# Turning four x tiles by one DMA and moving two v projections and one k projection in a fused attention and GEGLU kernel

## The chip, the cores and the metric

The kernel runs on one core of one Trainium2 chip. The metric is the device time of one execution in microseconds (us), lower is better. Most executions of one kernel lie within 0.3 to 0.4% of each other here, so most kernels were executed five times, in rounds shared with the kernel before on the same chip. All executions compared are in the fast state, with a granted clock of 1.0.

## The reference

Two branches share one input x of 2048 rows and 640 columns (bfloat16), and a gate mixes them.

```python
g = sigmoid((x * gate_w).sum(-1, keepdims=True))
# a: linear attention, 32 heads of 20 columns
q, k, v = split(x @ wqkv)                            # 640 x 1920
pq, pk  = q @ w_phi, k @ w_phi                       # per head, 20 x 20
phi_q   = concat(softmax(pq), softmax(-pq)); phi_k = the same of pk
kv = einsum(phi_k, v); z = sum(phi_k)
a  = ((phi_q @ kv) / (phi_q @ z + 1e-6)) @ wo
# b: GEGLU feed-forward, 1728 inner columns
b  = (gelu(x @ w_gate) * (x @ w_up)) @ w_down
out = g * a + (1 - g) * b
```

## The kernel before

It is one long hand-ordered program. TensorE (PE) multiplies; VectorE (DVE) and ScalarE (ACT) move results out of PSUM ("evict" them), whose banks 0 to 7 the program hands out by hand; SyncE (SP) issues nearly all DMAs. The 2048 rows are 16 tiles of 128 rows. Only the first 30 us matter here.

The projections read x transposed, from SBUF (`xT`). PE transposes tiles 0 to 3, transposing DMAs do the rest (`xturn(t, n)`: n tiles from tile t). w_phi is multiplied into the weights of k and q once ("folds"): for this, wk and wq come transposed as well (`wload`), and each of five folds of one weight is written to a pair of banks and evicted by DVE ("d") or ACT ("a").

The DMAs on SP's queue, in order of issue:

```python
xload("sp", 0); xload("sp", 2)                 # rows of tiles 0 to 3, plain
for kt in range(KD):                           # wv, five plain DMAs
    sc.dma("sp", ... self.w3[:, kt, 0:D] ...)
xturn(4, 2)
wload(self.wkT, D, "wkT")
xturn(6, 2)
wload(self.wqT, 0, "wqT")
xturn(8, 4)
xturn(12, 4)
# ... plain loads of w_gate, w_up, w_down, wo
```

The order of PE's work after v of tiles 0 to 3 (`ve(t, b)`: v of tile t into banks b, b+1, evicted by ACT; `ke`: k, followed by two exps on ACT; `f(kt, which, banks, engine)`: a fold):

```python
ve(4, 6)
ve(5, 0)
f(0, "k", (2, 3), "d")
f(1, "k", (4, 5), "a")
f(2, "k", (6, 7), "d")
f(3, "k", (0, 1), "a")
f(4, "k", (2, 3), "d")
ve(6, 4)
ke(0, 6)
self.k_sums(0)            # DVE: the softmax sums of tile 0, one TENSOR_REDUCE
ve(7, 0)
ke(1, 2)
f(0, "q", (4, 5), "d")
f(1, "q", (6, 7), "d")
ke(2, 0)
f(2, "q", (4, 5), "d")    # "the third q fold": needs banks 4, 5 of the first one back
f(3, "q", (2, 3), "d")
self.proj(3, 640, 384, 6, 128, ["wk2"])        # first half of k of tile 3
f(4, "q", (4, 5), "d")
self.proj(3, 1024, 257, 7, 0, ["wk2", "wgate"])
self.k_evac(3, 6)
self.k_scale(0)
self.k_norm(1)
self.pq(0, 1, 1, 0) ...   # pq = x @ folded wq
self.gram(0)              # phi_k^T v of tile 0, needs the scaled exps of tile 0
# ... then tiles 4 to 15: k (and v), pq, gram of an earlier tile
```

The softmax here doesn't subtract the row's maximum and nothing guards it: scores larger than these inputs give would overflow.

Of the kernel before, what the change touches and what calls it, by code (L numbers as in the profile page):

```python
# [107 lines left out]
class _Kernel:  # L108
# [99 lines left out]
    def loads(self):  # L208
# [10 lines left out]
        def wload(T, c0, key):  # L219
            sc.dma("sp", lambda e: e.dma_start_transpose(T[:, :, :], self.wqkv[:, c0:c0 + D]), writes=[key])  # L220

        def xturn(t, n):
            a, z = t * P, (t + n) * P
            sc.dma("sp", lambda e: e.dma_start_transpose(self.xT[:, :, a:z], self.x[a:z, :]),
                   writes=[("xT", k) for k in range(t, t + n)])
# [8 lines left out]
        xload("sp", 2)  # L234
        for kt in range(KD):
            sc.dma("sp", lambda e: e.dma_start(self.w3[:, kt, 0:D], w3[:, kt, 2 * D:3 * D]), writes=[("wv", kt)])
        xturn(4, 2)
        wload(self.wkT, D, "wkT")
        xturn(6, 2)
        wload(self.wqT, 0, "wqT")  # L240
        xturn(8, 4)
        xturn(12, 4)
# [308 lines left out]
    def attention_state(self):  # L551
        NT = self.NT
        order = [(b, i) for b in range(self.NB) for i in range(self.KD)]
        sc = self.sc
        ones = self.nc.const_aps.tensor(1.0, [P, 512], BF16)
        for n in (512, 512, 512, 512, 512, 512, 128, 128, 128):
            sc.op("pe", lambda e: e.matmul(self.bank(0, n), ones[:, 0:P], ones[:, 0:n], start=True, stop=True),  # L557
                  writes=[("ps", 0)])
        vs, ve, xt = self.v_step, self.v_first_evac, self.x_transpose
        xt(0, "d")  # L560
        xt(1, "a")
        for i in range(3):
            for a, b in ((0, 2), (64, 3)):
                sc.op("pe", lambda e: e.matmul(self.bank(b, P), ones[a:a + 64, 0:P], ones[a:a + 64, 0:P], start=True,  # L564
                                               stop=True), writes=[("ps", b)])
        xt(2, "d")
        xt(3, "a")
        for t in range(4):
            vs(t, 0)
        for t in range(4):  # L570
            vs(t, 1)
        for t in range(4):
            vs(t, 2)
        for t in range(4):
            vs(t, 3)
        self.blockdiag()
        self.gate_column(6)
        for t in range(4):
            vs(t, 4)
            ve([t], "ad"[t % 2], False)  # L580
            if t == 2:
                ve([0, 1, 2], "a", True)
        ve([3], "d", True)
        f = self.fold
        ve, ke = self.v_early, self.k_early
        ve(4, 6)
        ve(5, 0)
        f(0, "k", (2, 3), "d")
        f(1, "k", (4, 5), "a")
        f(2, "k", (6, 7), "d")  # L590
        f(3, "k", (0, 1), "a")
        f(4, "k", (2, 3), "d")
        ve(6, 4)
        ke(0, 6)
        self.k_sums(0)
        ve(7, 0)
        ke(1, 2)
        f(0, "q", (4, 5), "d")
        f(1, "q", (6, 7), "d")
        ke(2, 0)  # L600
        f(2, "q", (4, 5), "d")
        f(3, "q", (2, 3), "d")
        self.proj(3, 640, 384, 6, 128, ["wk2"])
# [5 lines that stand above are left out]
        self.pq(0, 1, 1, 0)  # L609
        self.pq(0, 0, 0, 1)  # L610
        self.pq(0, 3, 3, 2)
        self.columns = True
        self.gram(0)
        self.k_norm(2)
        self.pq(0, 2, 2)
        self.k_norm(3)
        n = 4
        g = 1
        for t in range(4, NT):
            if t < 8:  # L620
                self.k_early(t, 1)
            else:
                self.vk(t)
            self.k_norm(t)
            m = 2 * t - 2 if t < 8 else t + 5
            while n < m:
                if n == m - 1:
                    for g in range(g, t - 2):
                        self.gram(g)
                    g = t - 2  # L630
                self.pq(order[n][0], order[n][1], n)
                n += 1
# [242 lines left out]
```

## Time and profile before

| | before |
|---|---|
| median of 3 executions | 286.44 us (286.05 to 287.1) |
| span in the profile | 285.0 us |
| PE busy | 281.1 us, 99% |
| x tiles 4, 5 issued, landed, read | 4.10, 8.57, 10.8 us |
| wk issued, landed, read | 5.90, 12.84, 13.5 us |
| x tiles 6, 7 issued, landed, read | 9.45, 13.99, 15.3 us |
| sum of tile 0 on DVE | 19.72 to 21.20 us |
| third q fold starts | 22.77 us |

Landings are the time when the last of the increments of the DMA's semaphore arrives; the traces show sixteen for each of these DMAs (those of x tiles 4 and 5, for one, between 8.50 and 8.57 us). The page of the kernel before, its busy times and the chain of work that ended last:

```profile
...
PE 281.1 (99%) x3045; PEld 186.1 (65%) x3060; DVE 174.4 (61%) x352; ACT 105.2 (37%) x200; POOL 5.3 (2%) x36
...
PE 99%; issue 0%; ACT 0%
PE ps L361 62%; PE ps L737 28%; PE ps L681 2%; PE ps L373 2%; PE ps L468 2%; PE ps L341 1%; PE ps L557 1%; PE ps L298 0%; ACT outsb L750 0%; PE ps L564 0%; PE ps L323 0%
...
```

PE is the chain, from end to end. A busy PE isn't a full PE, because the profile models the ends of matmuls; so the thing to read is the distance between starts. In the stretch of interest 512-column matmuls start every 215 to 216 ns and 128-column ones every 55 ns. I call a "hole" what the distance between two starts has over that. Whatever delays PE here delays the end, unless it is made good later, and PE has hardly a hole in which to make it good.

The timeline of the kernel before (start in us, duration in us, engine, line, operation, out<-in, count; in brackets the idle time of the engine before it and what ended it). SPq is SP's sequencer issuing a DMA; the duration is that of the issue. L361 is a projection, L341 a fold, L438 the softmax sum, L354 the eviction of a fold. `ps` is PSUM, `xT`, `wkT`, `wqT` what the transposing DMAs bring, `BD` w_phi spread for the heads, `Ek` the exps of k, `Dk` their sums:

```profile
...
4.10 1.76 SPq L224 DMA_TRANSPOSE xT<-in_A_x_dram  x1
...
5.90 3.50 SPq L220 DMA_TRANSPOSE wkT<-in_A_wqkv_dram  x1
...
9.45 1.40 SPq L224 DMA_TRANSPOSE xT<-in_A_x_dram  x1
...
11.04 2.66 PE L361 MATMUL ps<-w,xT 128*128 128x512 bf16 x19
...
13.54 1.96 PE L341 MATMUL ps<-BD,wkT 128*128 128x140 bf16 x30
...
15.55 5.39 PE L361 MATMUL ps<-w,xT 128*128 128x512 bf16 x39
...
19.72 1.49 DVE L438 TENSOR_REDUCE Dk<-Ek 128x64 f32<-128x1280 bf16 x1 [3.29 <-ACT gcol L426]
...
20.78 0.79 PE L341 MATMUL ps<-BD,wqT 128*128 128x140 bf16 x12
...
21.36 1.56 DVE L354 CAST wq<-ps 128x640 bf16<-128x640 f32 x2 [0.16 <-PE ps L341]
...
22.77 0.79 PE L341 MATMUL ps<-BD,wqT 128*128 128x140 bf16 x12
...
25.33 3.19 PE L361 MATMUL ps<-xT,wq 128*128 128x512 bf16 x14
...
```

Neither a DMA nor an eviction is named as releaser before any PE group. (Some matmul records are missing, so a group can seem to start one matmul late, as at 11.04.) The sum of tile 0 is done at 21.20, and the first q eviction at 21.36 waits for PE. How long the first turning DMA took from issue to landing (view of one tile, `xT`, in the window of that issue; the three numbers of the first line are the duration of the issue in ns, those of the second the time to landing in us):

```profile
...
L224 SPq DMA_TRANSPOSE xT<-in_A_x_dram x1: 1760/1760/1760, 4.1 to 4.1; - x1
...
DMA to landing us min/median/max: 4.5/4.5/4.5
```

### The profile page before, as it was taken

To read this page: it belongs to the slowest core of one execution; us is meant where nothing else is said; L and a number is where in the kernel's file an instruction comes from. 1 tells how busy PE (TensorE), PEld (TensorE's weight loads), DVE (VectorE), ACT (ScalarE), POOL (GpSimd) and SP (SyncE) were. 2 spreads that over 40 slices of the span, in tenths; PEclk is the share of its full clock that TensorE was granted. 3 is DMA by queue.
4 is the path that set the end of the run, shared out by engine and by line. 5 is a ranking of instruction groups with operands and counts; after the bars stand their busy time and mean duration, and the time that the engine had idled before them with its cause. 6 is when DMAs were issued, how large, how long until landed. Compare 5 with 4: busy or idle time off the path is not lost.

```text
span 285.0 us, 7066 instructions
## 1 busy us (share of the span) xinstructions
PE 281.1 (99%) x3045; PEld 186.1 (65%) x3060; DVE 174.4 (61%) x352; ACT 105.2 (37%) x200; POOL 5.3 (2%) x36
## 2 busy tenths in 40 slices
PE   8999999999999999999999999999999999999996
PEld 4665799999984444444444444445777777777786
DVE  1459999999976652667242334225883883883801
ACT  4367898667754223222322223221112112112021
POOL 7000000000000000000000000000000000000000
DMA  8999993000002000011000000000233223322421
GB/s 228 225 199 313 361 349 111 2 0 2 2 0 48 0 0 2 2 23 25 0 0 0 2 0 0 0 2 0 26 82 58 50 62 59 70 52 68 71 72 48
DMA packets 36937, 18.67 MB, mean 66 GB/s; under 512 B 28970, under 2 KB 36394, under 8 KB 36906
## 3 DMA queue, kind: packets, MB, share of 16 engines
q1 hardware_dynamic: 36240, 18.19, 26.3%
q8 instruction: 24, 0.39, 0.6%
q10 hardware_dynamic: 666, 0.03, 0.2%
q14 instruction: 7, 0.06, 0.1%
HBM read 9.04 MB, written 2.62 MB: 41 GB/s over the span
## 4 chain that ended last, share of the span: by engine, by line
PE 99%; issue 0%; ACT 0%
PE ps L361 62%; PE ps L737 28%; PE ps L681 2%; PE ps L373 2%; PE ps L468 2%; PE ps L341 1%; PE ps L557 1%; PE ps L298 0%; ACT outsb L750 0%; PE ps L564 0%; PE ps L323 0%
## 5 line engine op out<-in xcount | busy, mean ns | idle before, releaser
L361 PE MATMUL ps<-xT,wg_sb 128*128 128x512 bf16 (+1 forms) x265 | 63.8, 379 | 0.4 <-issue 0.2
L361 PE MATMUL ps<-xT,wu_sb 128*128 128x512 bf16 (+1 forms) x263 | 63.3, 379 | 0.4
L653 ACT ACTIVATE gl<-ps 128x512 bf16<-128x512 f32 x52 | 30.9, 596 | 72.9 <-PE ps L361 70.7
L655 DVE TENSOR_TENSOR hT<-ps,gl 128x512 bf16<-128x512 f32 x39 | 26.6, 689 | 38.8 <-PE ps L361 38.7
L737 PE MATMUL ps<-wd_sb,hT 64*128 64x320 bf16 x648 | 48.5, 296 | 0.0
L361 PEld LDWEIGHTS ps<-xT,wu_sb 128*128 128x128 bf16 (+1 forms) x270 | 26.6, 99 | 29.5
L361 PEld LDWEIGHTS ps<-xT,wg_sb 128*128 128x128 bf16 (+1 forms) x270 | 26.2, 99 | 29.0 <-ACT gl L653 0.2
L361 PE MATMUL ps<-w,xT 128*64 128x512 bf16 (+6 forms) x398 | 41.5, 325 | 0.1
L750 ACT ACTIVATE outsb<-ps,Gm 128x320 bf16<-128x320 f32 (+2 forms) x31 | 14.5, 515 | 72.4 <-PE ps L737 72.4
L737 PEld LDWEIGHTS ps<-wd_sb,hT 64*128 64x128 bf16 x648 | 31.1, 94 | 12.2 <-issue 0.4
L361 PEld LDWEIGHTS ps<-w,xT 128*64 128x64 bf16 (+1 forms) x400 | 35.9, 107 | 4.5
L737 PE MATMUL ps<-wo_sb,goT 64*128 64x320 bf16 (+2 forms) x340 | 26.5, 288 | 0.0
L361 PE MATMUL ps<-xT,wq 128*64 128x512 bf16 (+1 forms) x184 | 26.0, 380 | 0.1
L438 DVE TENSOR_REDUCE Dk<-Ek 128x64 f32<-128x1280 bf16 x16 | 23.7, 1478 | 3.7 <-ACT gcol L426 3.7
L452 DVE TENSOR_TENSOR Ek<-Ek,Dk 128x640 bf16<-128x640 bf16 x32 | 25.0, 821 | 0.6
L708 DVE TENSOR_TENSOR O<-ps,RH 128x640 bf16<-128x640 f32 x32 | 24.7, 815 | 0.0
L423 ACT ACTIVATE Ek<-ps 128x640 bf16<-128x640 f32 x32 | 20.7, 703 | 4.2 <-PE ps L361 4.2
L537 ACT ACTIVATE Eq<-ps 128x512 bf16<-128x512 f32 x40 | 21.6, 607 | 0.6 <-PE ps L361 0.4
L655 DVE TENSOR_TENSOR xT<-ps,gl 128x512 bf16<-128x512 f32 x13 | 9.0, 690 | 18.2 <-PE ps L361 18.2
L737 PEld LDWEIGHTS ps<-wo_sb,goT 64*128 64x128 bf16 x340 | 16.0, 94 | 5.3
L361 PEld LDWEIGHTS ps<-xT,wq 128*64 128x64 bf16 (+1 forms) x185 | 15.4, 108 | 2.9
L737 PE MATMUL ps<-wd_sb,xT 64*128 64x320 bf16 (+2 forms) x270 | 16.0, 269 | 0.0
(71 smaller groups left out, 173.8 us busy)
## 6 DMA issues: line engine op xcount, KB each, us to landing
out_dram<-outsb SPq DMA_DIRECT2D x7, 320.0 KB, 2.3
wd_sb<-in_B_w_down_dram SPq DMA_DIRECT2D x1, 2080.0 KB, 12.9
wg_sb<-in_B_w_gate_dram SPq DMA_DIRECT2D x1, 1120.0 KB, 7.4
wu_sb<-in_B_w_up_dram SPq DMA_DIRECT2D x1, 1120.0 KB, 9.8
wg_sb<-in_B_w_gate_dram SPq DMA_DIRECT2D x1, 960.0 KB, 9.1
wu_sb<-in_B_w_up_dram SPq DMA_DIRECT2D x1, 960.0 KB, 9.3
w<-in_A_wqkv_dram SPq DMA_DIRECT2D x5, 160.0 KB, 3.6
wo_sb<-in_A_wo_dram SPq DMA_DIRECT2D x1, 800.0 KB, 8.5
```

The costliest lines, as they stand in the source:

```text
L361: self.sc.op("pe", lambda e: e.matmul(self.ps[a:z, bank * 512 + c0:bank * 512 + c0 + n], lhs[:, a:z], rhs, start=first, stop=fin), reads=r ...
L373: sc.op("pe", lambda e, c0=c0, n=n, bk=bk, col=col: e.matmul(self.bank(bk)[:, col:col + n], self.xT[:, kt, t * P:(t + 1) * P], self.w3[:, ...
L423: self.sc.op("act", lambda e, s=s, scale=scale: e.activation(self.Ek[:, se, s, :], self.ps[:, o:o + self.D], AF.Exp, scale=scale), reads=[ ...
L438: sc.op("dve", lambda e: e.tensor_reduce(self.Dk[:, se, 0, :].rearrange("p (s h) -> p s h", h=H), self.Ek[:, se, :, :].rearrange("p s (h d ...
L452: sc.op("dve", lambda e, v=v, r=r: e.tensor_tensor(v, v, r, ALU.mult), reads=[("Rk", se)], writes=[("Ek", se, s)])
L468: sc.op("pe", lambda e: e.matmul(self.ps[a:a + 64, b * 512 + c:b * 512 + c + 2 * nf], va[:, lo:lo + 64], self.Ek[:, se, :, f0:f0 + nf], st ...
L537: sc.op("act", lambda e, s=s, scale=scale: e.activation(self.Eq[:, s, i, b * self.BT:(b + 1) * self.BT], self.bank(bank), AF.Exp, scale=sc ...
L653: sc.op("act", lambda e: e.activation(self.gl[:, slot, :], self.bank(banks[0]), AF.Gelu_apprx_tanh), reads=[("ps", banks[0])], writes=[("g ...
L655: sc.op("dve", lambda e: e.tensor_tensor(hT, self.bank(banks[1]), self.gl[:, slot, :], ALU.mult), reads=[("ps", banks[1]), ("gl", slot)], ...
L708: dve(lambda e, o=o, f=f, s=s: e.tensor_tensor(o, V[s][:, :, :, 0:DH], f, ALU.mult), rb + [key(6 + s)], [("O", s, sl)], guard=old)
L737: sc.op("pe", lambda e: e.matmul(self.bank(bk, w), lhs, rhs, start=opens and x == 0, stop=end and not opens, skip_group_check=True), reads ...
L750: sc.op("act", lambda e: e.activation(dst, self.bank(bk, w), AF.Copy, scale=g), reads=rd, writes=wr)
```

## The change

The intent: x tiles 4 to 7 come by one transposing DMA ahead of wk. With tile 6 there early, its v can run ahead of the k folds, so that wk may land 1.36 us later without PE waiting; v of tile 7 covers the last eviction of the folds; keys 0 and 1 then follow each other.

```diff
-        xturn(4, 2)
+        xturn(4, 4)
         wload(self.wkT, D, "wkT")
-        xturn(6, 2)
         wload(self.wqT, 0, "wqT")
...
         ve(4, 6)
         ve(5, 0)
-        f(0, "k", (2, 3), "d")
-        f(1, "k", (4, 5), "a")
-        f(2, "k", (6, 7), "d")
-        f(3, "k", (0, 1), "a")
-        f(4, "k", (2, 3), "d")
-        ve(6, 4)
-        ke(0, 6)
+        ve(6, 2)
+        f(0, "k", (4, 5), "d")
+        f(1, "k", (6, 7), "a")
+        f(2, "k", (0, 1), "d")
+        f(3, "k", (2, 3), "a")
+        f(4, "k", (4, 5), "d")
+        ve(7, 6)
+        ke(0, 0)
         self.k_sums(0)
-        ve(7, 0)
         ke(1, 2)
```

## The prediction

> **What bounds the kernel.** The chain of waits gives 99% to TensorE (PE), so I read start-to-start times of its matmuls in the timeline. From 10.8 to 25.1 us (projections of v and k, folds of wk and wq) 512-column matmuls start every 215 to 216 ns, 128-column ones every 55 ns[...]. So PE is full except for short holes: 0.07 us before the fourth and 0.13 us before the fifth k fold (PSUM banks not yet evicted), 0.02 us before the last q fold. No operand is late: wk lands at 12.84 us (DMA issues and landings), read at 13.49; x tiles 6 and 7 land at 13.99, read at 15.3; wq lands at 17.98, read at 20.67.
>
> **What the change does.** Matmuls, evictions and bytes stay; one DMA fewer.
> - v of tile 6 (1.36 us of PE) moves ahead of the folds. That makes room for a later wk, which was not late.
> - x tiles 4 to 7 come in one DMA. Tiles 4 and 5 landed at 8.57 us; from issue times and the rate of packets I estimate 9.8 us for all four (at worst 10.7). They are needed at 10.76. wk should land at about 13.3, read at 14.85.
> - The k folds begin at 14.90 instead of 13.54 us. Their bank pattern relative to the evictions is as before, so the 0.2 us of holes stays.
> - k of tile 0 runs at 18.05 to 19.41 us instead of 16.70 to 18.06. The q folds start at 20.78 as before.
>
> **What it costs.** The sum over Ek of tile 0 (VectorE, 1485 ns) precedes the q-fold evictions in VectorE's program. Before, it ran at 19.72 to 21.20 and the first q eviction started at 21.36, held only by PE. Now k of tile 0 ends 1.36 us later, so the sum runs at about 21.08 to 22.56. [...]the first q eviction starts at about 22.55. The third q fold (same banks 4, 5) wants to start at 22.77; in the fifth k fold PE restarted 0.88 us after the start of the eviction it waited for, so it starts at about 23.43: a hole of 0.66 us. The first half of k of tile 3 (bank 6) then waits 0.1 us more; later waits fit. VectorE's following chain (98% busy to 80 us) shifts by 0.73 us, PE by 0.74, so later margins of gram (0.7 to 1.6 us) stay.
>
> **On the critical path:** all of it; PE is full afterwards. Gain: none. Sum: +0.74 us (0.3%). Predicted 287.15 us, range 286.6 to 287.7. Chances: faster by over 2% 0.003, within 2% 0.99, slower 0.007.
>
> **What would show it.** Right: the sum of tile 0 starts near 21.1 us; the third q fold starts near 23.4 after a hole of 0.5 to 0.8 us, ended by a VectorE wq eviction; from there everything is 0.7 us later; x tiles 4 to 7 land before 10.7. Wrong: no such hole, or one at 10.8 us (late x) or before the k folds (late wk).
>
> **What would make it wrong.** Transposing DMAs show pauses of up to 1.4 us in their packets (10.76 to 12.18 us); one hitting x tiles 4 to 7 would add up to 0.5 us. If unprofiled runs had wk late before, the change would gain instead.

That the eviction waits for the sum ahead of it in VectorE's program (a start at 22.55 us for a sum that ends at 22.56) was my assumption at that point. The "up to 0.5 us" at the end is an estimate too: in the trace of before, packets of transposing DMAs that began at 10.76 us took 1.42 us, and 9.8 plus 1.4 is 0.44 us behind the need at 10.76.

## The result, and the profile after

The changed kernel takes 287.78 us (median of 6 executions, 287.41 to 288.63), the kernel before in the same rounds 286.56. The ratio is 1.0046 with a 95% interval of 1.0027 to 1.0066. Ratios here and below are the mean time of one kernel's fast runs over that of the other's of the same rounds, so not quite the ratio of the medians. 1.0046 of 286.5 us is 1.3 us. That is within 2%, as predicted, but it is nearly twice the 0.74 us forecast, and the median lies just outside the range of 286.6 to 287.7.

The page of the changed kernel, the same parts:

```profile
...
PE 282.4 (98%) x3060; PEld 185.9 (65%) x3060; DVE 174.4 (61%) x352; ACT 105.3 (37%) x200; POOL 5.3 (2%) x36
...
PE 94%; DMA 3%; SPq 1%; issue 0%; DVE 0%; ACT 0%; DVEq 0%
PE ps L360 61%; PE ps L736 28%; DMA xT<-in_A_x_dram 3%; PE ps L680 2%; PE ps L467 2%; PE ps L340 1%; SPq L236 1%; DVE wq L353 0%; SPq L216 0%; ACT outsb L749 0%; DVEq L42 0%
...
```

The chain now runs through a DMA (3%, the turned x) and shows traces of DVE. The timeline of the changed kernel, same stretch (its lines are numbered one lower than before: L360 for L361, L340 for L341, L437 for L438, L353 for L354):

```profile
...
4.09 4.69 SPq L224 DMA_TRANSPOSE xT<-in_A_x_dram  x1
...
8.83 4.14 SPq L220 DMA_TRANSPOSE wkT<-in_A_wqkv_dram  x1
...
12.42 4.25 PE L360 MATMUL ps<-w,xT 128*128 128x512 bf16 x30 [1.14 <-DMA xT<-in_A_x_dram]
...
16.50 1.95 PE L340 MATMUL ps<-BD,wkT 128*128 128x140 bf16 x30
...
18.29 4.25 PE L360 MATMUL ps<-w,xT 128*128 128x512 bf16 x30
...
22.38 0.79 PE L340 MATMUL ps<-BD,wqT 128*128 128x140 bf16 x12
...
22.68 1.49 DVE L437 TENSOR_REDUCE Dk<-Ek 128x64 f32<-128x1280 bf16 x1 [3.29 <-ACT gcol L425]
...
24.08 3.83 DVE L353 CAST wq<-ps 128x640 bf16<-128x640 f32 x5
...
24.95 0.80 PE L340 MATMUL ps<-BD,wqT 128*128 128x140 bf16 x12 [0.42 <-DVE wq L353]
...
27.37 1.89 PE L360 MATMUL ps<-xT,wq 128*128 128x512 bf16 x8
...
```

Two brackets are new. v of tile 4 (12.42) waited for the DMA of x, and the third q fold (24.95) for the eviction of a q fold on DVE. The view of waits of PE from 10 to 36 us of the changed kernel (total us, times, longest) has just these two lines; the same view of the kernel before has none:

```profile
...
PE ps L360 <- DMA xT<-in_A_x_dram: 1.1, 1, 1.1
PE ps L340 <- DVE wq L353: 0.4, 1, 0.4
```

These idle times are counted from the modelled end of the matmul before, so they are smaller than the holes: the distance between starts is 1374 ns where 69 were due, a hole of 1.30 us, and 690 ns where 110 were due, a hole of 0.58 us. And the one DMA of x in the changed kernel:

```profile
...
L224 SPq DMA_TRANSPOSE xT<-in_A_x_dram x1: 4690/4690/4690, 4.1 to 4.1; - x1
...
DMA to landing us min/median/max: 8.3/8.3/8.3
```

The issue alone takes 4.69 us, and the landing comes 8.3 us after its start, at 12.37 us. Tiles 4 and 5 had landed at 8.57 before.

The sum for these two profiles closes. The spans differ by 2.24 us (287.24 against 285.00): 0.29 us because a load of x rows in front happened to land later (5.01 instead of 4.66 us), 1.30 us in the hole for x, 0.58 us in the hole at the third q fold and 0.07 us soon after it. From the first pq on, all is 2.25 us later to the end. The profiled execution of the changed kernel is, however, the slowest of its six (288.63 us). So in most executions x (or the head) probably costs less than in this trace. That is why the experiments below rest on times and traces together.

### The profile page after: what moved, and what is told of

It reads as the page before. It is cut to its first block, busy times and chain, and to the rows that moved or that the text cites. A ratio compares the mean times of both kernels' runs of the same rounds, so it can differ in the third digit from the quotient of the medians.

```text
span 287.2 us, 7078 instructions
## 1 busy us (share of the span) xinstructions
PE 282.4 (98%) x3060; PEld 185.9 (65%) x3060; DVE 174.4 (61%) x352; ACT 105.3 (37%) x200; POOL 5.3 (2%) x36
## 4 chain that ended last, share of the span: by engine, by line
PE 94%; DMA 3%; SPq 1%; issue 0%; DVE 0%; ACT 0%; DVEq 0%
PE ps L360 61%; PE ps L736 28%; DMA xT<-in_A_x_dram 3%; PE ps L680 2%; PE ps L467 2%; PE ps L340 1%; SPq L236 1%; DVE wq L353 0%; SPq L216 0%; ACT outsb L749 0%; DVEq L42 0%
## 5 line engine op out<-in xcount | busy, mean ns | idle before, releaser
L360 PE MATMUL ps<-xT,wg_sb 128*128 128x512 bf16 (+1 forms) x270 | 64.9, 379 | 0.0
L360 PE MATMUL ps<-xT,wu_sb 128*128 128x512 bf16 (+1 forms) x270 | 64.8, 379 | 0.0
L360 PEld LDWEIGHTS ps<-xT,wu_sb 128*128 128x128 bf16 (+1 forms) x270 | 26.6, 99 | 29.5
L360 PEld LDWEIGHTS ps<-xT,wg_sb 128*128 128x128 bf16 (+1 forms) x270 | 26.2, 99 | 29.0 <-ACT gl L652 0.2
L360 PE MATMUL ps<-w,xT 128*64 128x512 bf16 (+6 forms) x400 | 41.9, 325 | 1.1 <-DMA xT<-in_A_x_dram 1.1
L360 PEld LDWEIGHTS ps<-w,xT 128*64 128x64 bf16 (+1 forms) x400 | 35.8, 107 | 6.0 <-DMA xT<-in_A_x_dram 1.5
L360 PE MATMUL ps<-xT,wq 128*64 128x512 bf16 (+1 forms) x185 | 26.2, 380 | 0.0
L437 DVE TENSOR_REDUCE Dk<-Ek 128x64 f32<-128x1280 bf16 x16 | 23.7, 1480 | 3.6 <-ACT gcol L425 3.6
L451 DVE TENSOR_TENSOR Ek<-Ek,Dk 128x640 bf16<-128x640 bf16 x32 | 25.0, 822 | 0.6
L360 PEld LDWEIGHTS ps<-xT,wq 128*64 128x64 bf16 (+1 forms) x185 | 15.4, 108 | 2.8
## 6 DMA issues: line engine op xcount, KB each, us to landing
wu_sb<-in_B_w_up_dram SPq DMA_DIRECT2D x1, 960.0 KB, 10.1
wo_sb<-in_A_wo_dram SPq DMA_DIRECT2D x1, 800.0 KB, 10.1
```

Of the source, the lines that this page charges most:

```text
L360: self.sc.op("pe", lambda e: e.matmul(self.ps[a:z, bank * 512 + c0:bank * 512 + c0 + n], lhs[:, a:z], rhs, start=first, stop=fin), reads=r ...
L437: sc.op("dve", lambda e: e.tensor_reduce(self.Dk[:, se, 0, :].rearrange("p (s h) -> p s h", h=H), self.Ek[:, se, :, :].rearrange("p s (h d ...
L451: sc.op("dve", lambda e, v=v, r=r: e.tensor_tensor(v, v, r, ALU.mult), reads=[("Rk", se)], writes=[("Ek", se, s)])
```

## The experiments

Three theories for the missing half were set against each other. T1: the change has two separate costs, late x tiles and a late sum of tile 0 that holds the third q fold. T2: the sum is all, and the late x of one profile is an accident. T3: the DMA is all. The runs in one table, the holes in us from the start times in each trace (besides the 0.2 us before the k folds that the kernel before has too):

| run | median us | before, same rounds | ratio (95%) | x 4 lands | hole before v of 4 | hole before third q fold | other hole |
|---|---|---|---|---|---|---|---|
| changed | 287.78 | 286.56 | 1.0046 (1.0027 to 1.0066) | 12.37 | 1.30 | 0.58 | |
| changed again | 287.83 | 286.52 | 1.0040 (1.0026 to 1.0053) | 11.92 | 1.25 | 0.58 | |
| DMA part only | 287.98 | 286.84 | 1.0040 (1.0027 to 1.0053) | 11.08 | 0.22 | none | 1.75, k folds |
| order part only | 288.40 | 286.84 | 1.0060 (1.0048 to 1.0073) | 9.19 | none | 0.58 | 1.05, v of 6 |
| two turns | 287.26 | 286.84 | 1.0017 (1.0003 to 1.0031) | 8.85 | none | 0.58 | |
| sum, gram 0 late | 287.85 (four fast ones) | 286.84 | 1.0037 (1.0023 to 1.0051) | profile slow | | | |
| the same again | 287.49 | 286.52 | 1.0033 (1.0020 to 1.0045) | 11.22 | 0.29 | none | 0.53, gram 1 |
| short sum | 286.92 | 286.52 | 1.0016 (1.0003 to 1.0029) | 12.04 | 0.97 | none | |
| two turns, short sum | 286.64 | 286.52 | 1.0005 (0.9992 to 1.0017) | 8.73 | none | none | 0.32, k folds |
| two turns, sum and grams late | 286.77 | 286.91 | 0.9999 (0.9987 to 1.0012) | 8.96 | none | none | |
| plain DMA behind x | 287.94 | 286.91 | 1.0037 (1.0021 to 1.0052) | 11.53 | 0.49 | 0.58 | |
| plain DMA, sum and grams late | 287.49 | 286.91 | 1.0022 (1.0008 to 1.0036) | 12.04 | 0.60 | none | |
| more warming matmuls | 287.76 | 286.76 | 1.0033 (1.0016 to 1.0050) | 11.93 | 1.19 | 0.58 | |

### The DMA part only

```diff
 (kernel before)
-        xturn(4, 2)
-        wload(self.wkT, D, "wkT")
-        xturn(6, 2)
+        xturn(4, 4)
+        wload(self.wkT, D, "wkT")
```

> Only the DMA part: x tiles 4 to 7 in one transposing DMA ahead of wk, the order of the matmuls as in the kernel before. Theory T1 (two separate costs: the x tiles land late, and the sum of tile 0 holds the third q fold): x lands between 10.8 and 12.4 us where v of tile 4 wants it at 10.8, so a hole of 0.1 to 1.5 us there; wk lands between 14.0 and 15.7 where the folds, delayed with v, want it at 13.6 to 14.9, so a second hole of 0.5 to 0.8 us; no hole above 0.1 us before the third q fold. In sum 0.6 to 2.1 us slower than before. Rival T2 (the sum alone costs all of it, and the late x of the one profile is an accident): as before within 0.3 us.

It is 0.40% slower (1.1 us). Waits of PE from 10 to 36 us:

```profile
...
PE ps L340 <- DMA wkT<-in_A_wqkv_dram: 1.6, 1, 1.6
PE ps L360 <- DMA xT<-in_A_x_dram: 0.3, 1, 0.3
```

Late x and late wk hold PE, no eviction does. wk, now issued at 8.3 instead of 5.9 us, lands at 15.56. So the DMA part costs without the new order and its late sum. But most of that cost in this trace, a hole of 1.75 us, is late wk, which the new order makes harmless in the changed kernel; the hole for x is 0.22 us. What T2 calls an accident falls by other evidence: in all eight fast traces with one DMA of four tiles these land later than they are needed, and below, cutting the DMA in two shortens the time.

### The order part only

```diff
 (changed kernel)
-        xturn(4, 4)
-        wload(self.wkT, D, "wkT")
+        xturn(4, 2)
+        wload(self.wkT, D, "wkT")
+        xturn(6, 2)
```

> Only the order part: v of tile 6 ahead of the k folds, v of tile 7 behind, keys 0 and 1 in a row, with the DMAs of the kernel before. T1: x tiles 6 and 7 land at about 14.0 us where v of tile 6 wants them at 13.5, a hole of 0.4 to 0.5 us; the hole of 0.55 to 0.7 us before the third q fold stays, ended by a VectorE eviction. In sum 1.0 to 1.2 us slower than before. Rival T3 (all of the loss is the DMA's): as before within 0.3 us but for the late x 6.

It is 0.60% slower (1.7 us), more than the 1.0 to 1.2 us expected. Waits of PE:

```profile
...
PE ps L361 <- DMA xT<-in_A_x_dram: 0.9, 1, 0.9
PE ps L341 <- DVE wq L354: 0.4, 1, 0.4
```

The q fold waits as in the changed kernel, with DMAs that are not changed, so T3 falls. v of tile 6 waited 1.05 us rather than 0.45, because tiles 6 and 7 landed at 14.85 us in this execution, 0.86 later than in the trace of before. Landings of the same DMA list scatter by that much (0.61 us of it because the issue began later, at 10.06 instead of 9.45 us).

### Two turning DMAs instead of one

```diff
 (changed kernel)
-        xturn(4, 4)
+        xturn(4, 2)
+        xturn(6, 2)
         wload(self.wkT, D, "wkT")
```

> The changed kernel with its one DMA of four x tiles cut into two of two tiles, both ahead of wk. T1: tiles 4 and 5 land at about 8.6 us and tiles 6 and 7 before 13.5, no hole before v of tile 4; wk lands before 14.8; the hole of 0.55 to 0.7 us before the third q fold stays. 0.5 to 0.8 us slower than before. T2: as slow as the changed kernel, 1.2 us over before.

It is 0.17% slower than before (0.5 us), where the changed kernel is 0.40 to 0.46% slower. The waits of PE, and the two DMAs:

```profile
...
PE ps L341 <- DVE wq L354: 0.4, 1, 0.4
```

```profile
...
L224 SPq DMA_TRANSPOSE xT<-in_A_x_dram x1: 2039/2039/2039, 4.1 to 4.1; - x1
...
DMA to landing us min/median/max: 4.7/4.7/4.7
```

```profile
...
L224 SPq DMA_TRANSPOSE xT<-in_A_x_dram x1: 1808/1808/1808, 6.2 to 6.2; - x1
...
DMA to landing us min/median/max: 4.4/4.4/4.4
```

The first pair lands at 8.85 us and the second at 10.55; PE asks for tile 6 only at about 14. So the bytes ahead of wk are the same, and cutting the DMA in two takes the wait for x away. One expectation missed: wk landed at 15.31 us, not before 14.8, but PE asked for it at about 15.3, so that it cost less than 0.1 us. What is left is the q fold. The first issue starts at 4.10 us with one DMA as with two; what came sooner in the traces is the landing of tiles 4 and 5, 8.7 to 9.0 us in the three traces with two DMAs instead of 11.1 to 12.4.

### The sum moved behind the q folds

```diff
 (changed kernel)
         ke(0, 0)
-        self.k_sums(0)
...
         self.k_evac(3, 6)
+        self.k_sums(0)
         self.k_scale(0)
...
+        self.pq(0, 2, 2)
         self.gram(0)
         self.k_norm(2)
-        self.pq(0, 2, 2)
         self.k_norm(3)
```

> The changed kernel with the sum of tile 0 moved behind the q fold evictions on VectorE, and the gram of tile 0 moved behind one more pq so that it doesn't wait for the later sum. T1: no hole above 0.1 us before the third q fold, the late x stays: 0.1 to 1.5 us slower than before, about 0.6 us faster than the changed kernel. T2: as before within 0.3 us. T3: as slow as the changed kernel, 1.2 us over before.

One of the five executions, the profiled one, ran at a granted clock of 0.558 and took 498.7 us; it is left out and explains nothing:

```profile
...
core 0: 497.4 us, clock 0.558
...
```

The four fast ones were 0.37% slower than before, so the gain over the changed kernel was about 0.3 us or less, not 0.6. The kernel was run again, together with the changed kernel:

> The changed kernel once more, unedited, so that its time and trace stand on the same chip and in the same rounds as the next three: 1.0 to 1.5 us slower than before; hole of 0.58 us before the third q fold; x tiles 4 to 7 land between 10.8 and 12.4 us.

The changed kernel repeated itself: 1.0040, x landed at 11.92 us, the two holes as in the table.

> The changed kernel with the sum of tile 0 behind the q fold evictions and gram of tile 0 behind one more pq, once more, since its only profile fell in an execution at a granted clock of 0.56 and its fast runs gained only about 0.3 us over the changed kernel instead of 0.6. Mended theory T1: the hole before the third q fold is gone, but VectorE's chain is now the whole sum (1.5 us) later against PE, and the gram of tile 1, which had 1.0 us to spare, waits about 0.5 us for its scaling. Rival: the hole before the third q fold is still there, from something other than the sum.

Waits of PE in the second run:

```profile
...
PE ps L467 <- DVE Ek L451: 0.5, 1, 0.5
PE ps L360 <- DMA xT<-in_A_x_dram: 0.3, 1, 0.3
```

The mended theory holds. The eviction no longer holds the q fold, but DVE is 98% busy from 25 to 80 us (54.0 of the 55 us in the trace of the changed kernel), and the sum put into that chain makes everything behind it 1.5 us later against PE than in the kernel before. The gram of tile 1 then waits for its scaling (L451) with a hole of 0.53 us. The cost had moved, not gone.

### The sum made short (wrong result)

```diff
 (changed kernel, in k_sums)
-            self.Ek[:, se, :, :].rearrange("p s (h d) -> p s h d", d=DH), AX.X, ALU.add),
+            self.Ek[:, se, :, :].rearrange("p s (h d) -> p s h d", d=DH)[:, :, :, 0:2 if t == 0 else DH],
+            AX.X, ALU.add),
```

> The changed kernel with the sum of tile 0 cut short: 2 of every 20 columns are summed (a wrong result on purpose), all places and waits kept. T1: the sum takes about 0.2 instead of 1.49 us, the hole before the third q fold falls below 0.1 us and none comes back later: about 0.6 us faster than the changed kernel of the same rounds, the late x stays. Rival: what holds the third q fold is the late k of tile 0 on ScalarE, not the length of the sum; then the hole stays above 0.4 us.

The sum falls from 1.49 to 0.29 us. It is 0.16% slower than before, against 0.40% for the changed kernel in the same rounds: 0.7 us less. Timeline, then waits of PE:

```profile
...
22.05 0.79 PE L340 MATMUL ps<-BD,wqT 128*128 128x140 bf16 x12
...
22.34 0.29 DVE L437 TENSOR_REDUCE Dk<-Ek 128x64 f32<-128x128 bf16 x1 [3.29 <-ACT gcol L425]
...
22.63 1.56 DVE L353 CAST wq<-ps 128x640 bf16<-128x640 f32 x2
...
24.04 0.79 PE L340 MATMUL ps<-BD,wqT 128*128 128x140 bf16 x12
...
```

```profile
...
PE ps L360 <- DMA xT<-in_A_x_dram: 1.0, 1, 1.0
```

The first q eviction starts at 22.63 us, 0.58 after the start of the first q fold (22.05), and that is the distance in the kernel before too (20.78 to 21.36): PE sets it again, and that the short sum ends at 22.63 as well is chance. The third q fold no longer waits. In the changed kernel the distance is 1.70 us (22.38 to 24.08), 1.12 more, and the eviction starts as the sum ends (24.08 us, the recorded end of the sum being 24.16). The place and the waits of k of tile 0 were kept, so it is the length of the sum in front of the evictions that held the fold. In the changed kernel, then, an eviction whose input was ready waited 1.12 us for an unrelated sum ahead of it in VectorE's program. This pair of runs shows what the prediction assumed at this step.

### Both cut

```diff
 (kernel with the short sum)
-        xturn(4, 4)
+        xturn(4, 2)
+        xturn(6, 2)
```

> Both cuts at once: two DMAs of two x tiles ahead of wk, and the short sum of tile 0 (wrong result on purpose). T1: both holes gone, so the loss is accounted for: as before within 0.3 us. If a third cost is hidden in the change, it stays 0.4 us or more slower than before.

The ratio is 1.0005 (0.9992 to 1.0017): no different from before. The loss is accounted for by the two costs. One small wait is left in its trace, for wk, which landed at 15.18 us:

```profile
...
PE ps L341 <- DMA wkT<-in_A_wqkv_dram: 0.2, 1, 0.2
```

### A correct version without both costs

```diff
 (changed kernel with two turns, sum behind the q folds, gram 0 behind one more pq; and in the loop over tiles, for 4 to 7:)
             while n < m:
+                if n == m - 1 and t < 8:
+                    self.pq(order[n][0], order[n][1], n)
                 if n == m - 1:
                     for g in range(g, t - 2):
                         self.gram(g)
                     g = t - 2
-                self.pq(order[n][0], order[n][1], n)
+                if n < m - 1 or t >= 8:
+                    self.pq(order[n][0], order[n][1], n)
                 n += 1
```

> A correct version without both costs: two DMAs of two x tiles ahead of wk, the sum of tile 0 behind the q fold evictions, and in tiles 0 and 4 to 7 the gram behind the last pq of its iteration, which gives each gram 1.08 us more for the later VectorE chain. T1: no hole before v of tile 4, before the third q fold or before the gram of tile 1; a hole of 0 to 0.4 us before the k folds (wk lands at about 15.2). As before within 0.4 us, about 0.4 us faster than the kernel with the sum moved alone. If the chain of VectorE stays too late, a hole of 0.2 us or more before a gram of tiles 1 to 4.

The ratio is 0.9999 (0.9987 to 1.0012). The view of waits of PE has no line at all from 10 to 36 us; that of the weight loads has two; the first stands where PE turns to 64-column matmuls, where the distance is 309 ns in every kernel, the second made a hole of 24 ns:

```profile
...
PEld ps L361 <- ACT Eq L537: 0.4, 1, 0.4
PEld ps L341 <- DVE wq L354: 0.2, 1, 0.2
```

It equals the kernel before and doesn't beat it. It is also about 1.0 us better than the kernel with only the sum and gram moved (1.0033), where 0.4 was expected, if one compares ratios across rounds. No run beat the kernel before, as there was next to nothing to win: before the change PE had holes of only 0.2 us in this stretch.

### Why the one DMA landed late

The semaphore updates in the traces show the sixteen increments of a DMA one by one. They come in two groups. For x tiles 4 to 7 (us from the start of the span):

```
kernel          issue ends  first increments     last increments      16 KB packet of the instruction queue
changed         8.79        8 at 10.76 to 10.84  8 at 12.06 to 12.37  10.12 to 11.26
changed again   8.31        5 at 10.24 to 10.41  11 at 11.60 to 11.92 9.67 to 10.80
short sum       8.40        6 at 10.32 to 10.45  10 at 11.71 to 12.04 9.72 to 10.84
sum late again  7.64        6 at 9.55 to 9.70    10 at 10.93 to 11.22 9.11 to 10.18
DMA part only   8.27        8 at 10.26 to 10.34  8 at 10.94 to 11.08  13.35 to 14.53
```

The first group starts 1.9 to 2.0 us after the end of the issue, and alone would have been in time or nearly so (10.8 us is the need). The second starts 0.6 to 1.3 us after the first group's end. One idea was that the next transposing DMA, the one of wk, holds it.

```diff
 (changed kernel)
         xturn(4, 4)
+        g3 = self.wg.rearrange("(kt p) n -> p kt n", p=P)
+        sc.dma("sp", lambda e: e.dma_start(self.wgu_sb[:, :, 0:64], g3[:, :, 13 * P:self.F]), writes=["wgu0"])
         wload(self.wkT, D, "wkT")
... (moved from here, behind the loads of the first halves of w_gate and w_up)
-                sc.dma("sp", lambda e: e.dma_start(self.wgu_sb[:, :, 0:64], g3[:, :, 13 * P:self.F]), writes=["wgu0"])
```

> The changed kernel with one plain DMA (80 KB of w_gate, needed only much later) put between the DMA of x tiles 4 to 7 and the one of wk. In the traces so far a transposing DMA that another transposing one follows often completes in two groups of increments, the first 1.9 to 2.0 us after the end of its issue, the second only about when the packets of the next one flow (x tiles 4 to 7: 10.2 and 11.6 us); the last of them, with a plain DMA behind it, completes at once, 2.0 us after its issue. Theory A (the follower holds the second group): x lands by about 10.5 us, hole before v of tile 4 below 0.2 us, 0.3 to 0.8 us faster than the changed kernel. Theory B (the four tile DMA itself is slow): x lands at 11 to 12.4 us as before, no gain.

> The same plain DMA behind the one x DMA, with the sum and the grams moved as in the version with two DMAs. Under theory A as before within 0.4 us, with x by about 10.5 us; under theory B 0.3 to 1.0 us slower than before.

The idea was half right in the trace and brought nothing in time. With the plain DMA behind it, 15 of the 16 increments came by 9.98 us (issue ended at 7.86), and the last one came at 11.53:

```profile
...
L224 SPq DMA_TRANSPOSE xT<-in_A_x_dram x1: 3754/3754/3754, 4.1 to 4.1; - x1
...
DMA to landing us min/median/max: 7.4/7.4/7.4
```

v of tile 4 still had a hole of 0.49 us (in the first trace, too, it started at 12.42, behind the last increment at 12.37 and not behind the first eight at 10.84), and the ratio stayed at 1.0037; the second kernel, with the sum and the grams moved as well, came to 1.0022, where 1.000 was expected of the idea. That second kernel gives the cleanest test of the one DMA, in the same rounds: the correct version above has two turning DMAs in place of its one (and the plain DMA further down) and is 0.66 us faster on average, without overlap (286.68 to 287.07 against 287.11 to 287.73). What did go with the last increment in these traces is a packet of 16 KB on a queue that the profile calls "instruction". In the nine traces where it lies at 9.1 to 10.1 us, x tiles 4 to 7 (or, with two turns, 6 and 7) land 1.0 to 1.2 us after its end; in the DMA-part run it lies at 13.35 to 14.53 us, x lands at 11.08 and wk, the next, at 15.56, again 1.0 us after the packet. The traces of before and of the changed kernel have 24 such packets each, and 6105 and 6120 recorded PE instructions (matmuls and weight loads); between the starts of two packets lie 191 to 323 of these, about 255 in the mean. On this count alone I took the packets for PE's program; more is not shown. The last run was to move the packet, by the nine matmuls of constants that open the program ("warming" is no more than their name here; what they do to the clock was not tested):

```diff
 (changed kernel)
-        for n in (512, 512, 512, 512, 512, 512, 128, 128, 128):
+        for n in (128,) * 27:
```

> The changed kernel with its nine warming matmuls (six of 512 and three of 128 columns) cut into 27 of 128 columns: the same PE time, 36 PE instructions more. In all traces packets of 16 KB on an instruction queue come once per about 256 PE instructions, so they are taken for PE's program; the first of them lies at 9.1 to 10.1 us in six traces in which x tiles 4 to 7 land at 11.2 to 12.4 us, always 1.0 to 1.2 us after that packet's end, and at 13.35 us in the one (the DMA part alone) in which x lands at 11.08. Theory F (that packet holds the last of x): it moves about 2 us ahead, to 7 to 8.5 us, x lands by 11.1 us, the hole before v of tile 4 falls to 0.4 us or less, 0.2 to 0.9 us faster than the changed kernel, so 0.4 to 1.1 us slower than before. Rival: the packet only coincides; x lands at 11.2 to 12.4 us wherever the packet lies.

The edit didn't do what it was for. The packet stayed at 9.66 us though 36 PE instructions were added ahead, and x landed at 11.93, again 1.1 us after its end. Waits of PE:

```profile
...
PE ps L360 <- DMA xT<-in_A_x_dram: 1.0, 1, 1.0
PE ps L340 <- DVE wq L353: 0.4, 1, 0.4
```

So this tells nothing for or against. That this packet delays x is a coincidence seen in these traces, not a cause shown; it stays open, and so does what splits the increments in the DMA-part run, where no such packet is near.

The kept traces hold more on this, on both sides. Counted from the end of the issue, the landing takes 3.5 to 3.7 us in the nine traces with the packet near, and 2.8 and 2.6 us in the two without (the DMA part, and the second DMA of the two turns). A second packet at 23.8 to 24.9 us meets the DMA of x tiles 12 to 15 in five traces: in three of them (both cut, the correct version, more warming matmuls) the last increment alone comes 1.5 us behind the others, 1.1 us after the packet's end, in the other two it doesn't. And the scatter of the landing at 11.2 to 12.4 us is that of the issue, which took 3.55 to 4.69 us. In all eight fast traces this issue ended within 0.3 us after the last of the five plain wv loads ahead of it had landed (7.6 to 8.5 us). Whether these loads hold the issue was not tested. Nor is it known what sets the time of the packet: the DMA part has the same PE program as the kernel before, where it lies at 10.43 to 11.37 us and not at 13.35.

## Why the prediction was right or wrong

- **The cost of the sum: right.** Forecast: a hole of 0.66 us before the third q fold and 0.1 us soon after, together 0.74 us on the chain. Measured: 0.58 and 0.07 us in the traces, and 0.7 us between the changed kernel and the one with the short sum. The forecast start of the sum, 21.1 us, becomes 22.68 in the first trace, because x and the head made it 1.6 us later; the distance to k of tile 0 is as forecast.
- **The k folds: right.** The same holes are there, 0.07 and 0.13 us, at 17.5 and 18.0 us.
- **x tiles 4 to 7: the step that failed, the time of the one turning DMA.** "From issue times and the rate of packets I estimate 9.8 us for all four (at worst 10.7). They are needed at 10.76." They landed at 11.1 to 12.4 us in all eight fast traces with one DMA of four tiles, and PE waited 0.2 to 1.3 us at v of tile 4, where the prediction had no wait at all. The issue took 3.5 to 4.7 us where I had taken 3.45 from the later turns, and from its end to the landing it took 2.8 to 3.7 us, where the rate of packets let me take about 2.25 (2560 packets of 256 bytes, at about 1130 per us while they flow in the trace of before). The trace of before had a better measure, though not a sufficient one: its DMAs of x tiles 8 to 11 and 12 to 15, the same size, took 6.5 and 5.5 us from issue to landing, which would have put this one at 10.6 or 9.6. The first leaves 0.15 us of margin, and I named it as the worst case; the 7.0 to 8.3 us that this DMA took are longer than either. Why it takes longer in this place is open. And the risk at the end of the prediction, pauses of the turning DMAs worth "up to 0.5 us", may have been the right thing with too small a number; that a pause of this kind is what made x late is not shown.
- **The range: too narrow.** Its upper edge, 0.55 us over the middle, left no room for a late DMA, though the times of landing are what scatters in this kernel.
- **What the times say of the sizes.** The changed kernel lost 1.15 to 1.3 us. The short sum gives back 0.7 of it. Cutting the DMA gives back 0.3 us with the short sum (there 0.3 us of wait for wk come in) and 0.65 to 0.85 us without it, comparing ratios across rounds; the pair in the same rounds with the sum and the grams moved gives 0.66. The profiled executions of the changed kernel were the slowest of their rounds, so the hole of 1.3 us is probably not the typical one.

## What to carry to other kernels

Before you hide a wait, check that it exists: here wk was 0.65 us early in the trace, so that giving it 1.4 us more could win nothing, and each thing moved to make room took away someone else's margin. When work is moved on a full PE, follow what it feeds: a projection 1.36 us later made a sum later, and the evictions behind that sum in program order held PE (0.58 us). The DMA that joined two here served its first reader as late as its last (tiles 4 and 5 at 11.1 to 12.4 us instead of 8.57), so merge only those whose readers come at the same time; and leave it a margin. Here a rate gave 9.8 us, two DMAs of the same size and kind in the trace of before gave 9.6 and 10.6, and it came at 11.1 to 12.4.

## What the traces give on the DMAs, the packets and the clock

- From issue to landing, from DRAM, the transposing DMAs took, in the fast traces: 256 rows of 640 columns 4.4 us (two turns) to 5.4 us (the correct version), 512 rows 5.4 to 8.3 us (both in the changed kernel), a 640 by 640 weight 6.6 us (wq, changed kernel) to 7.3 us (wk, two turns).
- The sequencer's time to issue them is not small beside that: 3.27 to 4.69 us for 512 rows in the traces of before and of the changed kernel, half or more of the time to landing (4.69 of 8.3 us, 3.46 of 5.5 us), and the next DMA of the queue is issued behind it (8.83 us, after an issue from 4.09 to 8.79).
- The sixteen increments of one turning DMA often came in two groups 0.6 to 1.3 us apart (the table of increments above), or with a single straggler 1.5 us behind (both cut, the correct version, more warming matmuls).
- A 16 KB packet of the instruction queue takes 0.88 to 1.43 us in the traces of before and of the changed kernel, and in the nine traces where the first one began at 9.1 to 10.1 us, the turning DMA of x in flight landed 1.0 to 1.2 us after its end. That it delays them is not shown.
- One of the executions here, on a single core, had a granted clock of 0.56 in every stretch from 12 us to its end (0.558 in the mean of the view) and took 498.7 us.
